# Batch 0 through the same half-size products as the other batches, its values in a tile of their own, and every step from one ordered list

## The chip, the cores and the metric

The kernel runs on one core of a Trainium2 chip, in one launch. The metric is the device time of that core in microseconds; the time before is the median of three runs. Profiles show one execution of the program, recorded by the hardware profiler. Engines: PE (TensorE matmuls; PEld its weight loads), DVE (VectorE), ACT (ScalarE), POOL (GpSimd, which also issues every load from device memory), SP (SyncE, which issues stores, copies inside SBUF and DMA transposes).

## The reference

A sparse attention over 4 batches, 8 heads, 768 tokens and 64 columns per head, then a feed-forward layer with a quick gelu (512 to 2048 to 512):

```python
k_sum = k.reshape(B, H, nb, block, D).max(axis=3)      # block 32: 24 blocks
v_sum = v.reshape(B, H, nb, block, D).mean(axis=3)
scores_l = scale * q @ k.T ; mask_l = abs(i - j) < 16
scores_s = scale * q @ k_sum.T + log(block)
a = softmax(concat([where(mask_l, scores_l, -1e9), scores_s]))
x = a @ concat([v, v_sum])                             # heads side by side: 3072 x 512
h = x @ w_in
out = (h * sigmoid(1.702 * h)) @ w_out
```

So each token attends to at most 31 neighbours and to 24 block summaries.

## The kernel before, in words

**Engines in order.** Every instruction goes through `_Ordered`, whose `call` (line 28) keeps it in program order on its engine. Nearly all rows of the profile therefore carry line 28, and groups are told apart by tile names. What stands first in the program stands first on its engine's queue.

**Layout.** A batch is 768 tokens in two halves of 384. Heads go in four pairs p. Keys of a pair lie turned in `kx` as 12 tiles of 128 columns: 64 own keys, 24 block maxima, 32 neighbours' keys, padding. Values lie in `vw` in the same 128 rows. `kx`, `qT` and `vw` exist twice, for even and odd batches. A pair's scores for one half are twelve matmuls into `ps_s` (a double PSUM bank), an exponential on ACT into `a_sb`, a mask product on DVE with `mk`; its values are twelve matmuls into `ps_av`, a reciprocal and a product on DVE into `x`; `x` is turned into `xT` by PE (`tx`, tile `ps_x`) or by a DMA transpose (`dx`).

**Values' rows.** The neighbours' rows of `vw` are copied from other rows of `vw` by SP (`halo_dmas`: four copies), the 24 block sums from `vs` by two more (`sum_dmas`). The sums come from matmuls with a selector `E` into `ps_vs` and five DVE instructions (`block_sums`).

**Feed-forward.** `ph` = 4 matmuls of 384 columns per 128 of the 2048 hidden units and half; ACT applies the gelu into `gT`. For batches 1 to 3 the second layer uses the Strassen-Winograd form: seven half-size products instead of eight, in `product`, eight matmuls of 256 columns each, for three row tiles t. Its left operands are `gT` and the sums `gs` (`g_sums`, four DVE instructions per column tile and batch), its right ones `w_out` and the differences `ws` (`w_sum`). Products gather in banks `poA`, `poB`, `poC`; copies `s` and results `osb` leave on DVE and ACT, and SP stores `osb`.

**Batch 0.** Half 0 starts from special tiles while loads are still coming: whole 128-key tiles for own keys (`s_own`), separate small matmuls for neighbours (`s_edges`) and blocks (`b_turn`). Then come its 16 hidden tiles (`ff_in`, first two by `ff_first`), and its second layer as plain full products (`ff_out`, tile `po`, 16 matmuls of 512 columns for each row tile). Half 1's scores and values stand between these (`beside0`), then half 1's hidden tiles with the turning of batch 1's keys and queries (`tk`, `tq`, tile `ps_t`), then its `ff_out` with batch 1's attention between. Its values are loaded straight into `vw[0]` by eight DMAs, the second half of q by eight more (`load_q1`).

**Loads.** POOL issues all loads in order; at most eight are under way, since each waits for the eighth before it. Batch 1's loads stand behind the masks and w_out, batch b+2's behind the first product of batch b's second layer or, for batch 2, behind batch 0's. Keys and queries of batches 2 and 3 are turned by DMA transposes on SP (`xk`, `xq`), after which DVE takes the block maxima (`rest_k`, tile `ks`) and fills the neighbours' and maxima's columns of `kx`.

**PSUM.** Eight banks: `pmm`, four single ones, and `psb`, two double ones, each pool handing out its buffers in turn. Ahead of them, for the start, three other pools of two.

**Order of the work around.** Batch b+1's attention stands between the products of batch b by hand-made tables, for example

```python
plan = {-1: ["s00", "s01"], 2: ["m00", "m01"], 3: ["s02", "s03"], 5: ["m02", "m03", "s10", "s11"],
        7: ["m10", "m11", "s12", "s13"], 9: ["m12", "m13"], 10: ["v00", "v01"], 11: ["d00"], ...}
```

where a number is a place among the products and s, m, v, d are scores, mask, values and the transpose of a half and a pair. The activation table is switched between the exponential and the gelu by `exp_soon` and `gelu_soon`.

## Time and profile before

| | |
|---|---|
| runs | 213.35, 217.09, 213.35 us; median 213.35 |
| the profiled execution | 215.52 us, of which the profile's span is 213.8 |
| granted TensorE clock | 1.0 throughout |
| matmuls | 2359, PE busy 203.4 us (95%) |
| DVE, ACT, POOL busy | 127.2, 122.6, 97.6 us |
| DMA | 27.74 MB in 99690 packets, 89280 of them under 512 B |
| activation table loads | 10, 1283 ns each |

A group's row gives the line, engine and operation, output and inputs, shapes and count; then the busy us, the mean ns of one, and the engine's idle time just before them with what ended it. Matmuls overlap, so a mean is longer than the distance between two. A timeline row gives start, length, engine and group. In the slices each digit is a fortieth of the span, 9 for 90% or more.

### The profile page before, as it was taken

Reading aid. Unit: us, or ns where it says so; the run is one execution under the profiler, and the core shown is the slowest. Engines: PE = TensorE matmul, PEld = TensorE weight load, DVE = VectorE, ACT = ScalarE, POOL = GpSimd, SP = SyncE. Lnnn points to the kernel's source line nnn. Section 1 sums busy time; section 2 is a strip of 40 time slices with the busy share of each in tenths; the row PEclk is TensorE's granted clock in tenths of the full one; section 3 lists DMA queues with packets and bytes.
Section 4 is the critical chain, followed back from the end, with each engine's and each line's share of the span. In section 5 each row is a group of like instructions: output and inputs, shape, how many; then the busy total and the mean of one; then the engine's idle time right before and its main releaser. Section 6 shows DMA issues by size and latency. Waiting matters only on the chain.

```text
span 213.8 us, 5822 instructions
## 1 busy us (share of the span) xinstructions
PE 203.4 (95%) x2359; PEld 138.1 (65%) x2359; DVE 127.2 (59%) x384; ACT 122.6 (57%) x233; POOL 97.6 (46%) x156
## 2 busy tenths in 40 slices
PE   7899997999999999999699999999999999999993
PEld 2657564556664566665578876666788866668882
DVE  4565783455974693299885735996667615444111
ACT  2374778157849726776664248768671467772220
POOL 7998897379899989179369300000000000000000
PEclk9999999999999999999999999999999999999999
DMA  5999999999999999999999997943023820000222
GB/s 62 157 157 200 199 207 174 186 151 217 145 78 160 180 156 134 150 183 138 152 160 206 164 254 138 182 71 79 0 101 88 161 98 3 0 0 0 101 98 100
DMA packets 99690, 27.74 MB, mean 130 GB/s; under 512 B 89280, under 2 KB 96720, under 8 KB 99664
## 3 DMA queue, kind: packets, MB, share of 16 engines
q0 software_dynamic: 74032, 13.64, 82.2%
q1 hardware_dynamic: 25632, 13.74, 31.2%
q8 instruction: 18, 0.29, 0.6%
q14 instruction: 8, 0.07, 0.1%
HBM read 27.26 MB, written 6.29 MB: 157 GB/s over the span
## 4 chain that ended last, share of the span: by engine, by line
PE 52%; DMA 17%; POOL 14%; DVE 10%; issue 3%; ACT 2%; POOLq 0%; DVEq 0%
PE ph L28 21%; PE poA L28 13%; PE poB L28 6%; DMA w_out_sb<-in_moe_w_out_dram 5%; POOL qb L28 5%; POOL vw L28 4%; DMA kx<-kb 4%; PE po L28 4%; DVE gs L28 4%; PE poC L28 4%; DMA w_in_sb<-in_moe_w_in_dram 3%; DMA qb<-in_q_dram 3%; PE ps_av L28 2%; POOL mk L28 2%; PE ps_s L28 2%
## 5 line engine op out<-in xcount | busy, mean ns | idle before, releaser
L28 PE MATMUL ph<-xT,w_in_sb 128*128 128x384 bf16 x512 | 86.4, 326 | 0.5 <-DVE xT L28 0.5
L28 ACT ACTIVATE gT<-ph 128x384 f16<-128x384 f32 x128 | 61.3, 491 | 25.9 <-PE ph L28 25.7
L28 PEld LDWEIGHTS <-w_in_sb 128*128 128x128 bf16 x512 | 49.3, 98 | 31.8 <-issue 0.6
L28 PEld LDWEIGHTS <-gT 128*128 128x128 f16 x312 | 29.2, 98 | 12.4 <-issue 0.7
L28 POOL DMA_DIRECT2D vw<-in_v_dram x44 | 31.5, 758 | 6.4 <-PE ps_s L28 1.7
L28 ACT ACTIVATE a_sb<-ps_s 128x768 bf16<-128x768 f32 x32 | 24.3, 806 | 15.1 <-PE ps_s L28 15.0
L28 PEld LDWEIGHTS <-gs 128*128 128x128 f16 x288 | 27.5, 98 | 4.6 <-issue 1.2
L28 DVE TENSOR_TENSOR gs<-gT 128x384 f16<-128x384 f16 x48 | 17.0, 354 | 22.0 <-ACT gT L28 21.9
L28 POOL DMA_DIRECT2D kb<-in_k_dram x28 | 22.9, 841 | 11.8 <-DMA kx<-kb 5.6
L28 POOL DMA_DIRECT2D qb<-in_q_dram x34 | 27.4, 839 | 1.6 <-DMA vw<-in_v_dram 1.1
L28 PE MATMUL po<-w_out_sb,gT 128*128 128x512 f16 x96 | 22.8, 380 | 0.0
L28 DVE TENSOR_TENSOR a_sb<-a_sb,mk 128x768 bf16<-128x768 bf16 x28 | 14.9, 555 | 7.9 <-ACT a_sb L28 7.1
L28 PE MATMUL poA<-ws,gs 128*128 128x256 f16 x144 | 18.7, 273 | 0.8 <-DVE s L28 0.8
L28 DVE TENSOR_TENSOR x<-ps_av,rc 128x384 bf16<-128x384 f32 x32 | 17.8, 558 | 1.1
L28 DVE TENSOR_REDUCE ks<-kx 128x24 bf16<-128x768 bf16 x12 | 11.4, 948 | 7.4 <-DMA kx<-kb 4.0
L28 ACT ACTIVATE s<-poA 128x256 f32<-128x256 f32 x14 | 5.4, 385 | 17.8 <-PE poA L28 17.4
L28 ACT ACT_TABLE_LOAD x10 | 12.8, 1283 | 1.0 <-PEq L1069 0.8
L28 DVE RECIPROCAL rc<-ps_av 128x6 f32<-128x6 f32 x32 | 6.0, 189 | 8.2 <-PE ps_av L28 7.9
L28 DVE TENSOR_TENSOR osb<-poC,s 128x256 f32<-128x256 f32 x9 | 3.8, 423 | 11.8 <-PE poC L28 10.0
L28 PE MATMUL poA<-ws,gT 128*128 128x256 f16 x72 | 9.3, 272 | 0.4 <-DVE osb L28 0.4
L28 PE MATMUL poA<-w_out_sb,gT 128*128 128x256 f16 x72 | 9.4, 273 | 0.0
L28 PE MATMUL poB<-ws,gs 128*128 128x256 f16 x72 | 9.4, 273 | 0.0
(88 smaller groups left out, 205.8 us busy)
## 6 DMA issues: line engine op xcount, KB each, us to landing
out_dram<-osb SPq DMA_DIRECT2D x23, 256.0 KB, 3.4
kb<-in_k_dram POOLq DMA_DIRECT2D x24, 96.0 KB, 6.2
qb<-in_q_dram POOLq DMA_DIRECT2D x24, 96.0 KB, 5.7
vw<-in_v_dram POOLq DMA_DIRECT2D x36, 64.0 KB, 5.2
w_out_sb<-in_moe_w_out_dram POOLq DMA_DIRECT2D x4, 512.0 KB, 10.7
w_in_sb<-in_moe_w_in_dram POOLq DMA_DIRECT2D x3, 512.0 KB, 10.3
vw<-vs SPq DMA_DIRECT2D x6, 198.0 KB, 4.7
kb<-in_k_dram POOLq DMA_DIRECT2D x4, 192.0 KB, 5.3
```

What stands on the lines that cost most here:

```text
L28: r = f(*a, **kw)
```

## The change

1. **Batch 0's second layer** uses `product` like the others: both halves' hidden tiles first, then 21 half-size products. `g_sums` takes one or two column tiles at a time.
2. **Batch 0's values** are loaded by four DMAs into a tile `v0n`; DVE copies the rows that half 1 needs into `vw[0]` (`own0`). The late half of q is loaded as the early one is, three tokens to a row, by two DMAs, and turned by the same helper. Half 1's keys are laid out by instructions over all four pairs at once, some on POOL (`late_own`, `late_halos`, `late_rows`). The scores' mask is put into PSUM ahead of the scores (`s_mask`).
3. **PSUM** is six pools of one buffer, four single banks (0 to 3) and two double ones (4, 5), and every step names its bank; 40, 41, 50, 51 are halves of the double ones.
4. **Every step** stands in the string `ORDER`: a step's name, its numbers, its engine (d, a, g) or bank. The tables, the loops and `beside` go. Loads, copies, exponentials and sums are steps of their own; some copies out of PSUM move between DVE and ACT. The exp and gelu switches for batch 0 become one each.

```diff
-    pidle = first.enter_context(tc.tile_pool(name="pidle", bufs=2, space=bass.MemoryType.PSUM))
...
+    psum = [ctx.enter_context(tc.tile_pool(name=f"ps{i}", bufs=1, space=bass.MemoryType.PSUM)) for i in range(6)]
-    def load_q1(h):
...
-        pool.dma_start(out=qb2["late"][:, h // 2, :, h % 2],
-                       in_=q[0, h, HALF:S].rearrange("(a p) d -> p a d", p=128))
+    def load_q0(half, g):
...
+        pool.dma_start(out=qb2[half][:, 4 * g:4 * g + 4].rearrange("p h r d -> p h (r d)"),
+                       in_=q[0, 4 * g:4 * g + 4, half * HALF:half * HALF + HALF]
+                       .rearrange("h (p r) d -> p h (r d)", r=JH))
+    def load_v0(p):
+        pool.dma_start(out=v0n[:, 2 * p:2 * p + 2, :, 0:D].rearrange("p h j d -> p (h j) d"),
+                       in_=v[0, 2 * p:2 * p + 2].rearrange("h (j p) d -> p (h j) d", p=128))
+    def own0(e):
+        r = slice(64 * e, 64 * e + 64)
+        dve.tensor_copy(out=five(0)[r, JH - e:NJ, e, :, 0:D],
+                        in_=v0n[r, :, JH - e:NJ, 0:D].rearrange("p h j d -> p j h d"))
+    def late_own(e, eng):
+        flat = kxs[0].rearrange("p i t c -> p (i t c)")
+        kf = kn.rearrange("p i s -> p (i s)")
+        eng.tensor_copy(out=at(flat, 256 * JH + 192 * e, [[NQ * 128, NP], [256, JH], [1, 64]]),
+                        in_=at(kf, HALF + 64 * e, [[S, NP], [128, JH], [1, 64]]))
-    def ff_out(u, ms, part):
...
-            pe.matmul(out=po, lhsT=gT[u % 2][:, nt, ms * 128:(ms + 1) * 128],
-                      rhs=w_out_sb[:, nt, :], start=(nt == 0), stop=(nt == NT - 1))
```

Parts of the order around batch 0's half 1 (Q and Qc q turn and copy, s and e scores and exponential, f hidden tile, G the switch to gelu, g gelu, vo and vr own rows and sums, ha and sd SP's copies, m mask, v and n values, t and c turn of x), the middle of batch 0's products with batch 1's sums and the release of batch 2's loads (gate, lk, lv, lq), and the first steps of batch 1's hidden tiles with the transposes (xk, xq), key maxima (xm) and key copies (kh, kr):

```
f.0.0.k01.2 f.0.1.k01.3 Q.1.1.0 Qc.1.2.a Qc.1.3.d mf s.0.1.1.42 e.1.1 f.0.0.k23 s.0.1.2.52 e.1.2 f.0.2.k0123.1
f.0.1.k23 s.0.1.3.42 e.1.3 f.0.3.k0123.0 ... f.0.7.k0123.41 G g.0.0 g.0.1 g.0.6 g.0.7 vo.0 vo.1 vr ha.0.0.3
g.0.2 g.0.3 sd.0.0.3 g.0.4 ha.0.3.3 sd.0.1.3 m.1.0 ha.0.1.3 ha.0.2.3 ow.1 ck.1 ... f.0.8.k0123.2 m.1.1 m.1.2 m.1.3
g.0.8 f.0.9.k0123.3 g.0.9 f.0.10.k0123.1 g.0.10 v.0.1.0.40 v.0.1.1.41 n.1.0 n.1.1 f.0.11.k0123.0 g.0.11 v.0.1.2.50
...
p.1.5.1 x.1.5.a ha.1.0.0 ha.1.2.0 ha.1.3.0 vm.1.42 vb sd.1.0.0 sd.1.1.0 gate lk.2.0 lk.2.1 lv.2.2.0 lv.2.2.1 lv.2.3.0
lk.2.3 lv.2.5.0 lv.2.5.1 lk.2.2 lk.2.4 lk.2.5 ha.1.1.0 lk.2.7 lv.2.0.1 lv.2.0.0 lk.2.6 ...
g.0.9 xk.0.0.0 xk.0.0.1 xk.0.1.0 xk.0.1.1 xq.0.0 xq.0.1 f.1.0.k0123.2 g.1.0 ... gs.0.2.3 xm.0.0 kh.0.0.d kr.0.0.d ...
```

## The prediction

> **What bounds the kernel now.** I read the page's busy shares and slices first, then the costliest groups, then PE's timeline by stage, then the waits.

> ```profile
> PE 203.4 (95%) x2359; PEld 138.1 (65%) x2359; DVE 127.2 (59%) x384; ACT 122.6 (57%) x233; POOL 97.6 (46%) x156
> ...
> PE   7899997999999999999699999999999999999993
> ...
> PEclk9999999999999999999999999999999999999999
> DMA  5999999999999999999999997943023820000222
> ```

> TensorE is the bound: 203.4 of 213.8 us, always at the full granted clock. The DMA engines are full until 128 us. They do not stop PE, but a transfer issued in that time lands late.

> ```profile
> L28 PE MATMUL ph<-xT,w_in_sb 128*128 128x384 bf16 x512 | 86.4, 326 | 0.5 <-DVE xT L28 0.5
> ...
> L28 PE MATMUL po<-w_out_sb,gT 128*128 128x512 f16 x96 | 22.8, 380 | 0.0
> ...
> L28 PE MATMUL poA<-w_out_sb,gT 128*128 128x256 f16 x72 | 9.4, 273 | 0.0
> ...
> vw<-vs SPq DMA_DIRECT2D x2, 99.0 KB, 5.3
> ...
> vw<-vw SPq DMA_DIRECT2D x3, 49.5 KB, 5.7
> ```

> Matmuls overlap, so their mean ns is a latency. The cadence comes from the timeline's starts: 48 ph in 7.96 us are 0.163 each; 16 po in 3.63 are 0.217; eight poA start 0.873 after the eight before them, 0.109 each. The last two lines are copies inside SBUF for batch 0's second half, issued on SP; they land 5.3 and 5.7 us after issue.

> ```profile
> 21.79 0.87 PE L28 MATMUL ph<-xT,w_in_sb 128*128 128x384 bf16 x4
> ...
> 36.00 3.63 PE L28 MATMUL po<-w_out_sb,gT 128*128 128x512 f16 x16
> 39.56 0.57 PE L28 MATMUL ps_av<-vw,a_sb 128*64 128x65 bf16 x24
> ...
> 46.86 0.50 PE L28 MATMUL ps_x<-wide,x 128*128 128x128 bf16 x6
> ...
> 81.16 7.15 PE L28 MATMUL ph<-xT,w_in_sb 128*128 128x384 bf16 x43
> ...
> 105.61 1.03 PE L28 MATMUL poA<-ws,gs 128*128 128x256 f16 x8 [0.77 <-DVE s L28]
> ```

> Input products of half 0 start at 21.8. Half 1's values (ps_av) at 39.6 need the copies above, and 16 po hide their flight. At 47.2 half 1 is turned, with 40 of half 0's 48 po done. Batch 1's input products start at 79.5, its products at 102.9.

> ```profile
> DVE ks L28 <- DMA kx<-kb: 4.0, 1, 4.0
> ...
> PE ps_s L28 <- DVE vs L28: 0.9, 1, 0.9
> ...
> PE poA L28 <- DVE s L28: 0.8, 1, 0.8
> ...
> PE ps_vs L28 <- DMA vw<-in_v_dram: 0.5, 1, 0.5
> ```

> VectorE waits 4.0 us for the key transposes of batch 2, runs 14 us without a gap (91.0 to 105.1), and PE waits 0.9 and 0.8 at the end of that. These are most of PE's named waits after the start.

> **The change, part by part.** The sum is made against the profiled span of 213.8 us. That execution took 215.5; the runs shown have a median of 213.35, so differences are carried over to that median.

> *Products of batch 0.* 96 matmuls of 512 columns (96 x 0.217 = 20.8 us) become 7 x 8 x 3 = 168 of 256 (168 x 0.109 = 18.3): **-2.5**. VectorE gets batch 0's sums gs: six in pairs of 768 columns (the mask product of that size takes 0.555) and two single ones, 12 x 0.555 + 8 x 0.354 = 9.5 us, beside the 8 ws sums of 0.68 (5.5 us). They lie in half 1's input products, 16 x 0.65 + 3 x 0.33 = 11.4 us, with 2.1 us of product and turn cover (p.1.1, p.0.1, tk.3). 15.0 us of VectorE against 13.5 of cover: it overruns some 1.5, but product 5 needs only the first of the last sums. I take 0.3 on the path, bounds 0 and 1.5. Without the cover all 9.5 would be on it.

> *The start, to the point where batch 0's half 1 is turned.* The first DMAs keep their order, so the first half ends as before: last norm at 22.0 to 22.8 us. POOL now does kx copies (768 elements: from the 0.43 of its 288-element copy I take 0.9; in all 2.8 us) ahead of the third w_in load. They wait for the last turned keys (13.5) and maxima (17.8), not for the end, and end near 19; mask building follows and ends near 28 (its 27.3 before). So the first half-1 scores are not held, and input products start at 23.5 instead of 21.8, for a q turn, three x turns and a score group now stand ahead. Then to the end of the 11th input tile: 11 x 0.65 + q turn 0.46 + 3 score groups at 0.23 and 0.1 of entry each + 0.7 where the second q turn waits for the x copies behind an exponential = 9.3, that is 32.8. Here half 1's values want their rows. VectorE writes own rows and sums only after the last q copy (25.9): 0.68 + 0.9 + 4 x 0.24, done at 28.4. Behind that SP issues five more copies at 0.6 to 0.8 each (last one near 31.2), landing 5.2 to 5.8 later among the w_out loads: **36.8**. PE stands 4 us; its own queue, all the other input tiles, is behind it, and so are the two values' norms on VectorE and everything later. Then four value groups (1.1), five input tiles (3.25), two turns (0.66): 41.8. Before, 47.2 less the 40 po (8.7) is 38.5. So **+3.3**, bounds -0.7 (no wait) and +4.5 (w_in's third chunk 1 us late too).

> [...]

> *From there to batch 1's input products.* Work in both: 16 input tiles, 8 turns of k and q, sums, 8 score and 8 value groups, 3 x turns. Before, the extra over those sums is 79.5 - 47.2 - 30.4 = 1.9 (the 0.5 for the v load among it). After: 8 entries of 0.1, the 0.3 above, and 0.7 where values of batch 1 stand 6.3 us behind the sums whose copies need 1.5 on VectorE and 4.7 to land: 1.8. **-0.1**, bounds -1.9 and +2. The half-q loads in longer runs (2048 fewer packets) and four v loads instead of eight shorten the DMA queue; PE waited 0.5 and 1.1 on it, counted above, bounds 0 and -1.6.

> *Batch 1's products.* Before, 24.8 us for 18.3 + 1.85 + 1.8 of work. The first key transposes again stand behind a store, and batch 2's loads start at 66 (64.5 before), the keys now mixed with v loads (15th instead of 8th issue). They land near 91 as before. VectorE's 14 us shrink by 1.0, for its gs come in pairs, and copies out of PSUM move to ACT: **-0.9**, bounds 0 and -1.85 (both waits gone).

> *Batches 2 and 3.* The 0.2 waits for osb go with these moves: **-0.3**, bounds 0 and -1. PSUM: six pools with the same four single and two double banks, so no more buffering than before; the two table loads saved (10 to 8, 1.28 each) are on ACT, 57% busy: 0 on the path; without that cover 2.6. The tail is unchanged.

> Sum: -2.5 + 3.3 - 0.1 - 0.9 - 0.3 = **-0.5**, a span of 213.3 and a median of **212.9**.

> **The rivals.**

> *The rows for half 1 are there in time* (faster). If the SBUF copies land in 2.8 us, as batch 1's larger ones did by the DMA issues from 60 to 68 us, 2.9 of the 4 us go; if the q turn's wait, which holds up VectorE's rows, is missing, another 0.7; with the waits of batch 1 gone too (0.9) the time is 208.4. For it: a short first DMA queue. Against: all six copies of this very stage took over 5 us.

> *Batch 2's keys become the bound* (slower). Place: the four key transposes in batch 1's input products. VectorE needs 9.5 us after the last pair (two maxima with copies 3.0, sums gs 4.0, block sums 1.5, a first share of the last sums 1.0), and PE wants product 5 near 103.2. So it decides when the last pair lands after 93.7, and each us beyond is a us of PE, once in batch 1 and again in batch 2, whose loads are mixed in the same way. Loads drain 1.7 us later and the transposes are served with them; the last pair can be issued when the 15th load has landed (66.2 + 15 x 0.79 + 5.5 = 83.5), 2.5 apart by the longest issue, and lands 8.8 later by the slowest of them, near 94.8, and with the 1.7 near 96.5: 2.8 us twice, 218.5. For it: VectorE's 4.0 us wait above. Against: before, transposes issued from 80.6 to 86.0 overlapped.

> *The half-size products give nothing* (no change). If VectorE's sums for batch 0 cost the full 1.5 overrun and ACT's copies lag, the 2.5 are given back: 214 to 215. For it: 15.0 against 13.5. Against: PE's needs come in steps.

> **How the numbers follow.** My forecast has 0.38, the faster rival 0.31, the slower one 0.19, the third 0.12. A measurement of this kernel tells about 2% from no change, 4.3 us: under 209.1 is faster, over 217.6 slower. The forecast and the third case are within: 0.50. The faster rival gives 0.31, the slower 0.19. The forecast's own range, by the start's and the middle's bounds halved, is 210 to 216. To leave out no more than 2 in 10 the range must reach into both others: 206.5 (208.4 less the middle's lower bound, 1.9) to 218.0.

> **What would show it.** 168 more matmuls of 256 columns and no po row; PE idle of some 4 us ahead of the first ps_av with 64-column tiles, named after a DMA vw, near 33 us; input products from 23.5; half 1 turned near 42; batch 1's input products near 80, its products at 102 to 103. No such idle would prove the start wrong; a "DVE ks <- DMA kx" wait over 5 us, with PE waiting on gs, would prove the slower rival.

## The result, and the profile after

The changed kernel takes 221.41 us (median of 6 runs, 219.72 to 223.96) against 214.66 for the kernel before beside it (6 runs, 213.35 to 217.99): a ratio of 1.029, 95% interval 1.024 to 1.034. It is slower; 212.9 was forecast, and 221.4 lies above the range given. Ratios, here and below, leave out executions more than 1.5% above the fastest of their kernel; medians do not. The profiled execution took 222.04 us, its span is 220.1.

First the page of the changed kernel: busy time by engine, PE's busy tenths and PE's granted clock in 40 slices of 5.5 us, and the DMA share.

```profile
PE 203.4 (92%) x2416; PEld 145.7 (66%) x2416; DVE 135.3 (61%) x364; ACT 119.2 (54%) x233; POOL 93.6 (43%) x150
...
PE   7778893999999499999999998999999999999994
...
PEclk9999997699999959999999999999999999999999
DMA  6999999999907999999999999994011840000222
```

PE is as long busy as before although batch 0's products are 2.5 us less work, and there are two dents in its row (the 3, and the 4 in the middle), each with a dent of the clock in the same slice or the next. Before, the clock had none. The waits of PE name what makes the dents in its own row (us in total, times, longest):

```profile
PE ps_av L28 <- DMA vw<-vw: 7.7, 2, 4.0
```

PE's timeline (start, us, operation, tiles, count, idle time before it and what ended it) shows both places:

```profile
27.23 5.58 PE L28 MATMUL ph<-xT,w_in_sb 128*128 128x384 bf16 x32
36.78 0.96 PE L28 MATMUL ps_av<-vw,a_sb 128*64 128x65 bf16 x24 [3.97 <-DMA vw<-vw]
37.67 1.46 PE L28 MATMUL ph<-xT,w_in_sb 128*128 128x384 bf16 x4
...
73.57 0.22 PE L28 MATMUL ps_av<-vw,a_sb 128*64 128x65 bf16 x1
77.48 0.84 PE L28 MATMUL ps_av<-vw,a_sb 128*64 128x65 bf16 x23 [3.69 <-DMA vw<-vw]
78.25 1.89 PE L28 MATMUL poB<-ws,gs 128*128 128x256 f16 x8
...
88.46 1.46 PE L28 MATMUL ph<-xT,w_in_sb 128*128 128x384 bf16 x8
```

The first wait is the forecast one: half 1's values of batch 0, 3.97 us, ended at 36.78. The second stands at batch 1's first values, 3.69 us; before, PE reached these without a wait, at 71.42. Behind each, work runs at half speed: four `ph` in 1.40 us up to the next group (0.65 before), eight `poB` in 1.82 (0.87 before). Batch 1's input products start at 88.46, where 80.1 was forecast and 79.53 was the time before.

The granted clock in windows of 0.5 us (window, its length, busy us of PE, PEld, DVE, ACT, POOL, then PEclk, DMA share, GB/s):

```profile
35.50:36.00 0.50, 0.00 (x0) 0.00 (x0) 0.00 (x0) 0.00 (x0) 0.00 (x0) 0.63 1.22 236
36.00:36.50 0.50, 0.00 (x0) 0.00 (x0) 0.00 (x0) 0.00 (x0) 0.00 (x0) 0.50 1.23 205
...
42.00:42.50 0.50, 0.50 (x4) 0.25 (x3) 0.00 (x0) 0.00 (x0) 0.44 (x2) 0.54 2.41 153
...
76.50:77.00 0.50, 0.00 (x0) 0.00 (x0) 0.00 (x0) 0.00 (x0) 0.00 (x0) 0.59 1.31 279
...
83.00:83.50 0.50, 0.50 (x6) 0.44 (x5) 0.07 (x1) 0.23 (x1) 0.50 (x2) 0.58 2.04 129
```

The windows between these show 0.50, those outside 1.00. So a mean of 0.63 over 0.5 us is read as 0.13 us at 1.0 and the rest at 0.5: the clock falls at 35.63. Read alike, it is back at 42.46, falls at 76.59 and is back at 83.42. Each time it is low for 6.83 us, of which PE works 5.68 and 5.94: half of that, 2.8 and 3.0 us, is lost. So the waits cost 7.7 us and the low clock, called half clock below, 5.8.

What makes the second wait is on SP's queue:

```profile
65.54 0.88 SPq L28 DMA_DIRECT2D out_dram<-osb  x2
66.61 2.71 SPq L28 DMA_DIRECT2D vw<-vw  x3
69.43 1.27 SPq L28 DMA_DIRECT2D vw<-vs  x2
70.74 0.94 SPq L28 DMA_DIRECT2D vw<-vw  x1
```

The halo copies of batch 1 stand behind two stores that can only go at 65.5, when batch 0's first sums have left PSUM; the last halo stands behind the block sums' copies too and lands near 77.4. PE wants the rows at 73.8. Before, these copies stood ahead of the stores, and the values (first line) came 5 us behind the last one's issue:

```profile
71.42 0.57 PE L28 MATMUL ps_av<-vw,a_sb 128*64 128x65 bf16 x24
...
61.83 2.68 SPq L28 DMA_DIRECT2D vw<-vw  x4
64.61 1.56 SPq L28 DMA_DIRECT2D vw<-vs  x2
```

### The profile page after: what moved, and what is told of

Its sections match the earlier page's. It is cut to its first block, busy times and chain, and to the rows that moved or that the text cites. A ratio compares the mean times of both kernels' runs of the same rounds, so it can differ in the third digit from the quotient of the medians.

```text
span 220.1 us, 5893 instructions
## 1 busy us (share of the span) xinstructions
PE 203.4 (92%) x2416; PEld 145.7 (66%) x2416; DVE 135.3 (61%) x364; ACT 119.2 (54%) x233; POOL 93.6 (43%) x150
## 3 DMA queue, kind: packets, MB, share of 16 engines
q0 software_dynamic: 71824, 13.64, 77.9%
## 4 chain that ended last, share of the span: by engine, by line
PE 74%; DMA 13%; POOL 6%; DVE 3%; SPq 2%; issue 1%; ACT 0%; POOLq 0%; DVEq 0%
PE ph L28 36%; PE poA L28 17%; PE poB L28 9%; DMA vw<-vw 5%; DMA w_in_sb<-in_moe_w_in_dram 5%; PE poC L28 4%; PE ps_av L28 3%; DMA out_dram<-osb 3%; PE ps_s L28 2%; POOL v0n L28 2%; SPq L28 2%; POOL qb L28 1%; POOL kb L28 1%; PE ps_t L28 1%; PE ps_x L28 1%; DVE vs L28 1%
## 5 line engine op out<-in xcount | busy, mean ns | idle before, releaser
L28 PE MATMUL ph<-xT,w_in_sb 128*128 128x384 bf16 x512 | 88.0, 331 | 0.0
L28 ACT ACTIVATE gT<-ph 128x384 f16<-128x384 f32 x128 | 58.9, 494 | 33.6 <-PE ph L28 33.2
L28 PEld LDWEIGHTS <-w_in_sb 128*128 128x128 bf16 x512 | 49.6, 99 | 32.6 <-issue 1.6
L28 PEld LDWEIGHTS <-gs 128*128 128x128 f16 x384 | 37.0, 100 | 5.2
L28 DVE TENSOR_TENSOR gs<-gT 128x768 f16<-128x768 f16 (+1 forms) x40 | 18.5, 474 | 22.3 <-ACT gT L28 22.0
L28 POOL DMA_DIRECT2D kb<-in_k_dram x28 | 23.4, 841 | 18.4 <-DMA kx<-kb 9.9
L28 PEld LDWEIGHTS <-gT 128*128 128x128 f16 x288 | 27.6, 98 | 4.4 <-issue 0.8
L28 ACT ACTIVATE a_sb<-ps_s 128x768 bf16<-128x768 f32 x32 | 24.5, 808 | 5.5 <-PE ps_s L28 5.4
L28 POOL DMA_DIRECT2D vw<-in_v_dram x36 | 25.2, 759 | 2.2 <-DMA w_out_sb<-in_moe_w_out_dram 1.6
L28 PE MATMUL poA<-ws,gs 128*128 128x256 f16 x192 | 25.8, 279 | 0.0
L28 POOL DMA_DIRECT2D qb<-in_q_dram x28 | 23.2, 865 | 2.0 <-DMA vw<-in_v_dram 2.0
L28 ACT ACTIVATE s<-poA 128x256 f32<-128x256 f32 x18 | 6.9, 385 | 22.5 <-PE poA L28 20.1
L28 DVE TENSOR_TENSOR x<-ps_av,rc 128x384 bf16<-128x384 f32 x32 | 17.8, 558 | 1.1
L28 DVE TENSOR_TENSOR a_sb<-a_sb,mk 128x768 bf16<-128x768 bf16 x28 | 14.6, 553 | 3.7 <-ACT a_sb L28 3.6
L28 PE MATMUL ps_av<-vw,a_sb 128*64 128x65 bf16 x336 | 8.5, 210 | 7.7 <-DMA vw<-vw 7.7
L28 PEld LDWEIGHTS <-a_sb 128*64 128x64 bf16 (+1 forms) x360 | 8.3, 122 | 10.5 <-issue 9.4
L28 DVE RECIPROCAL rc<-ps_av 128x6 f32<-128x6 f32 x32 | 6.1, 189 | 14.3 <-PE ps_av L28 14.1
L28 PE MATMUL poB<-ws,gs 128*128 128x256 f16 x96 | 13.3, 285 | 0.0
L28 PE MATMUL poA<-ws,gT 128*128 128x256 f16 x96 | 12.4, 273 | 0.6 <-DVE osb L28 0.6
L28 POOL COPY kx<-kx 128x80 bf16<-128x80 bf16 (+1 forms) x12 | 3.5, 336 | 21.4 <-DMA kx<-kb 17.4
L28 PE MATMUL poC<-w_out_sb,gT 128*128 128x256 f16 x96 | 12.6, 274 | 0.0
L28 PE MATMUL poB<-w_out_sb,gs 128*128 128x256 f16 x96 | 12.5, 273 | 0.0
(95 smaller groups left out, 215.8 us busy)
```

The source lines that it names most:

```text
L28: r = f(*a, **kw)
```

## The experiments

All are copies of the changed kernel with words of the list moved, unless said otherwise. The ratio is that to the kernel before, with its 95% interval. T, T2, R1 and R2 are the theories that an expectation names. What is read from a profile is read from one execution.

### The waits, each and both, and the waits filled

**e1, batch 1's rows earlier.**

```diff
 e.0.1 p.0.3
+ha.1.0.0 ha.1.2.0 ha.1.3.0 ha.1.1.0 vm.1.42 vb sd.1.0.0 sd.1.1.0
 x.1.1.a ... o.0.0.0.0.2 ... o.0.0.1.0.2 ... x.1.5.a
-ha.1.0.0 ha.1.2.0 ha.1.3.0 vm.1.42 vb sd.1.0.0 sd.1.1.0
 gate ... lk.2.5
-ha.1.1.0
```

> Only the second wait is taken away: batch 1's block sums and its six in-SBUF row copies are issued ahead of batch 0's first stores (sums on TensorE one score group earlier). Theory T (the changed kernel loses its time in two TensorE waits for row copies, 4.0 and 3.7 us, and in the half clock of about 6 us that follows each, 2.6 us each): the idle of 3.7 us ahead of batch 1's values shrinks below 1 us, the granted clock there stays at 1.0, and the time is 6.3 us less than the changed kernel's, near 215. Rival R1 (the half clock has nothing to do with standing still): only 3.7 us go, near 217.7, and the half clock still shows near 77 us. Rival R2 (the time is lost in the half-size products and the single list, and the waits only move): within 2 us of the changed kernel.

Measured 219.87 us, ratio 1.020 (1.012 to 1.027). The second wait is gone, but the sums now stand ahead of other work on DVE, and PE waits 0.64 us for `vs` and 1.79 for `osb` a little earlier, with half clock from 68.25 to 71.67. The first wait is as it was (3.95 us). The test moved too much; m1 below moves less.

**e2, batch 0's rows earlier.** The memsets `ow.0 cv.0 cvs` go into DVE's time between 8.1 and 11.3 us, and:

```diff
 xc.0.a ... Q.1.0.42
+vo.0 ha.0.0.3 ha.0.1.3
 Qc.1.0.a Qc.1.1.d
+vo.1 ha.0.2.3 ha.0.3.3 vr sd.0.0.3 sd.0.1.3
 ... g.0.7
-vo.0 vo.1 vr ha.0.0.3
 g.0.2 g.0.3
-sd.0.0.3
 g.0.4
-ha.0.3.3 sd.0.1.3
 m.1.0
-ha.0.1.3 ha.0.2.3
```

> Only the first wait is taken away: VectorE clears batch 0's value tile in an idle gap before 13 us, and writes own rows and sums right after the first half's last norm, 3.4 us earlier, so that the six row copies are issued from 23.4 to 27.5 us instead of 26.8 to 31.9. Theory T: the copies land near 32.5 to 33, the idle of 4.0 us at 32.8 us is below 1 us, no half clock after it, and the time is 5.5 to 6.6 us less, near 215 to 216. R1: 3 to 4 us less, and a half clock still shows near 36 to 42 us. R2: within 2 us of the changed kernel.

Measured 215.83 us, ratio 1.002 (0.998 to 1.005). The first wait and its half clock are gone, and 5.6 us with them: most of what the change had lost. The second wait is now in two parts, on PE's timeline:

```profile
69.71 0.19 PE L28 MATMUL ps_av<-vw,a_sb 128*64 128x65 bf16 x1 [1.89 <-DMA vw<-vs]
71.39 0.84 PE L28 MATMUL ps_av<-vw,a_sb 128*64 128x65 bf16 x23 [1.49 <-DMA vw<-vw]
```

One matmul between them did not help: read from windows as above, the clock falls at 70.76 and is back at 77.59.

**e3, both edits together.**

> Both edits together. T: both idles and both stretches of half clock are gone, 12 to 13 us less than the changed kernel, near 208.5 to 209.5, and faster than the kernel before by 2 to 3%. R1: 7 us less, near 214, with half clock left. R2: 217 or more; and if batch 2's keys take over as the bound once the rest is earlier, 211 to 213 with a wait of VectorE for kx over 4 us.

Measured 216.87 us, ratio 1.011 (1.006 to 1.015): no better than e2, and 8 us above what T gave. No wait for row copies is left; others came, on PE's timeline:

```profile
58.74 0.25 PE L28 MATMUL ps_vs<-vw,E 64*32 64x128 bf16 x7 [0.46 <-DMA vw<-in_v_dram]
59.43 0.30 PE L28 MATMUL ps_vs<-vw,E 64*32 64x128 bf16 x16 [0.44 <-DMA vw<-in_v_dram]
...
61.38 0.78 PE L28 MATMUL ps_s<-qT,kx 64*128 64x64 bf16 x24 [0.66 <-DVE vs L28]
63.70 1.87 PE L28 MATMUL poB<-ws,gs 128*128 128x256 f16 x8 [1.54 <-DVE osb L28]
```

The sums now wait for batch 1's v loads, which land near 59.4, and DVE stands behind the sums. The clock falls at 61.47, after no single wait of more than 0.7 us.

**e4, the waits filled.** Seventeen matmuls of 512 columns on `w_in_sb` into a free bank ahead of `v.0.1.0.40`, fifteen ahead of `v.1.0.0.50`.

> The waits stay, but TensorE does not stand still in them: 17 products of 512 columns on data at hand (3.7 us, their results are used by nothing) ahead of batch 0's second-half values, 15 (3.3 us) ahead of batch 1's values. The row copies land when they did. T: granted clock 1.0 throughout, so 2.6 us less after each wait, 5 us in all, near 216, though not a word of the order is moved. R1: the clock still falls, time unchanged within 1 us, near 221. R2: no less, rather more than the changed kernel.

Measured 218.89 us, ratio 1.014 (1.006 to 1.022). PE's timeline at both places:

```profile
34.84 3.83 PE L28 MATMUL ps_h<-w_in_sb 128*128 128x512 bf16 x17 [0.34 <-ACT gT L28]
38.59 0.57 PE L28 MATMUL ps_av<-vw,a_sb 128*64 128x65 bf16 x24
...
72.70 3.40 PE L28 MATMUL ps_h<-w_in_sb 128*128 128x512 bf16 x15
76.03 0.57 PE L28 MATMUL ps_av<-vw,a_sb 128*64 128x65 bf16 x24
```

### Where the rest of the gain goes

**e5, all rows early, sums in place.** Batch 0's rows as in e2, and:

```diff
 x.0.3.a
+ha.1.0.0 ha.1.2.0
 o.0.0.0.0.2
+ha.1.3.0 ha.1.1.0
 x.0.4.a
-o.0.0.1.0.2
 ... x.1.5.a
-ha.1.0.0 ha.1.2.0 ha.1.3.0
 vm.1.42 vb sd.1.0.0 sd.1.1.0
+o.0.0.1.0.2
 gate ... lk.2.5
-ha.1.1.0
```

> From the kernel with batch 0's rows early (215.8 us, where TensorE still stands 1.9 and 1.5 us ahead of batch 1's values and 6.8 us of half clock follow): the four halo copies of batch 1 go ahead on SyncE's queue, two before and two after batch 0's first store, the sums stay where TensorE and VectorE make them. Theory T: the last copy is now one of the sums', issued near 64 us and landing near 69.5 to 70, where TensorE wants it at 67.8: a wait of 1.5 to 2 us is left. [...] R2 (nothing to be had from the rows): 215.8.

Measured 214.49 us, ratio 0.999 (0.995 to 1.003): level with the kernel before, and 0.5 above the 214 expected for a clock that falls at this wait too. Its profiled execution kept the clock at 1.0 over one wait, now for the sums, and took 213.72, where 211 to 212 were expected for a clock that holds:

```profile
70.04 0.56 PE L28 MATMUL ps_av<-vw,a_sb 128*64 128x65 bf16 x23 [2.62 <-DMA vw<-vs]
```

Four others had a mean clock of 0.992 and took 0.5 to 0.9 us more than it. The clock is not all: one at 0.999 took 215.51.

**e6, batch 1's first values two products later.** `p.2.5.1 x.2.5.a p.2.6 x.2.6.a` go ahead of `v.1.0.0.50`; turning and copying follow.

> The same, and batch 1's first values two products of batch 0 (1.75 us) later in TensorE's order, the transposes and their copies with them. T: no wait over 0.7 us from 25 us on, granted clock 1.0, and both the 3.4 us of waits and the 3.1 us of half clock of the kernel with batch 0's rows early are gone: 209 to 210.5, 2% or more under the kernel before. If batch 2's keys or sums take over as the bound now that all comes 6 us earlier, 211 to 212.5, with waits named after gs or vs near 100 us. R2: 215 or more.

Measured 217.07 us, ratio 1.009 (1.004 to 1.014), a clear miss. The wait is still 1.55 us, batch 1's input products start at 78.35 (e5: 78.38), and a new wait comes in batch 2, for a DMA transpose that lands late:

```profile
129.08 0.50 PE L28 MATMUL ph<-xT,w_in_sb 128*128 128x384 bf16 x2 [1.29 <-DMA xT<-x]
```

**e7, e6 with full products for batch 0.** All `gs` of batch 0 go; each `p` of batch 0 becomes 4 or 8 matmuls of 512 columns into `po`, and ACT copies `po` to `osb`.

> The same again, but batch 0's second layer as 96 full products of 512 columns instead of 168 half-size ones, copied out by ScalarE, and without VectorE's sums gs for batch 0 (8 ws sums stay). The computed output is the same. T: the half-size products are worth what the count of columns says, so this is 2.2 to 2.5 us slower than the kernel with values later, near 212. R2 (half-size products give nothing, since VectorE's 9.5 us of sums cost what TensorE gains): no difference, or faster.

Measured 217.29 us, ratio 1.011 (1.001 to 1.021): 0.2 above e6, not 2.2 to 2.5. Batch 1's input products start at 78.43 (e6: 78.35). PE has 2.5 us more to do there and waits 1.9 us less. Beside rows that come when they come, the half-size products buy waiting.

**m2, the changed kernel with full products for batch 0**, nothing else changed (as in e7).

> The changed kernel with the half-size products of batch 0 alone taken back: 96 full products of 512 columns, copied out by ScalarE, without VectorE's sums gs for batch 0 (the 8 ws sums stay); rows, queues and waits as in the changed kernel. TensorE reaches batch 1's values 1.8 us later (75.5 us), the block sums stand 0.9 us later. If the gain of the half-size products goes into the wait for the rows: the second wait falls by 0.9 us to 2.8, and batch 1's input products come 1 to 1.6 us later than the changed kernel's 88.5, not 2.5 later: 221 to 223. If they are worth their count: wait unchanged at 3.7 and 224.

Measured 219.81 us, ratio 1.023 (1.016 to 1.030): not slower than the changed kernel. The second wait:

```profile
75.92 0.54 PE L28 MATMUL ps_av<-vw,a_sb 128*64 128x65 bf16 x23 [1.09 <-DMA vw<-vw]
```

It is 2.6 us shorter: PE comes 1.0 later, and the last copy lands 1.6 earlier. That copy was issued at 70.9, in the changed kernel at 70.7, and took 4.9 us to land instead of 6.6; no run shows whether the products have a part in that. Behind it the clock stays at 1.0, and behind the first wait it is low from 37.47 to 40.88 only, which costs 1.7 us instead of 5.8 for both. So it is 61.4 us from the first to batch 1's input products, against 65.4: 2.5 more of work, 2.7 less waiting, 4.1 less lost to the clock. Why the clock was low for 3.41 us here and for 6.83 behind the changed kernel's first wait, no run shows; the other two cancel, with the help of that quicker copy. The cleaner pair is e6 and e7.

**m1, the halos alone on SP's queue.** The moves of e5 without those of e2; the second store goes behind the sums' copies.

> The changed kernel with one edit on SyncE's queue alone: batch 1's four halo copies go ahead, two before and two after batch 0's first store; its sums, its values and all of batch 0's rows stay. In the changed kernel the last halo copy stands behind two stores, three halos and both sums' copies, is issued at 70.7 us and lands at 77.4. Theory T: the sums' copies (70.7 us at the latest) are now last and land near 76.2, so the second wait falls from 3.7 to 2 to 2.7 us and the first (4.0 us, with its half clock) stays; the half clock behind the second comes in some runs only, as in the kernel with all rows early: 217.5 to 220. If the place of the halos on the queue is not what sets the second wait: 3.5 us of wait and 221.

Measured 221.51 us, ratio 1.027 (1.019 to 1.035). The wait is of the size T gave:

```profile
76.80 0.57 PE L28 MATMUL ps_av<-vw,a_sb 128*64 128x65 bf16 x23 [2.09 <-DMA vw<-vs]
```

So the place of the halos on SP's queue set 1.6 us of the second wait, and the sums' copies the rest. The median did not fall, and is what was expected if the halos' place did not matter. The profiled execution took 225.4 and is read for this stage only: batch 1's input products come 60.0 us after the first ones instead of 65.4, most of it by less half clock (3.4 us of it behind the first wait, none behind the second), and batch 2 gives the gain back in this execution, with 1.81 and 0.75 us of wait for `xT`. Where the others lost it was not seen.

**e9, e5 with nine products of 512 columns in the wait.**

> From the kernel with all rows early and the sums where they were (214.5 us; its profiled run at clock 1.0 stands 2.6 us ahead of batch 1's values): nine products of 512 columns on data at hand (2.0 us, results used by nothing) fill that wait, nothing else is changed. Its runs so far took 213.1 to 213.7 at a mean granted clock of 1.0, 214.2 to 214.6 at 0.992 and 215.4 to 216.9 at 0.984. [...]

If TensorE's idle time in that wait is what brings the clock down, nearly all runs were expected at 0.998 or above, with a median of 213.2 to 213.8 us; if it falls for another reason, the same spread of clocks and 214.5.

Measured 214.98 us, ratio 1.001 (0.996 to 1.006). The clock did what the first of these says: ten of its twelve executions had 0.997 or above, in e5 three of ten. The time did not: the profiled execution, at clock 1.0, waits 1.45 us for `vs` and 0.7 each for `gs` and `s` from 102 us on.

**e10, batch 1's q in two loads with long runs**, sums and rows half a product group earlier than in e5.

```diff
-lk.1.6 lq.1.0 lq.1.1 lk.1.7 lq.1.2 ... lq.1.7
+lk.1.6 lk.1.7 L4.0 L4.1
+pool.dma_start(out=qb2[g] (p h (r d)), in_=q[1, 4g:4g+4].rearrange("h (p r) d -> p h (r d)", r=NJ))
```

> Is the wait of 2.6 us that is left set by batch 1's loads, so that TensorE's gain from the half-size products can't come out? Batch 1's q is loaded by 2 DMAs of four heads in runs of six rows (1024 packets) instead of 8 DMAs in single rows (6144 packets), and put back in order by the copies out of PSUM; its block sums and rows are issued half a product group earlier, as that now finds its values landed. GpSimd issues 6 loads of 0.82 us less ahead of the values, so these land near 54.5 to 55 instead of 59.4, the rows near 66 to 67, where TensorE wants them at 67.4. If the loads set it (T): no wait over 0.7 us ahead of batch 1's values, batch 1's input products from 75.5 to 76 instead of 78.4, its products from 98 instead of 100.7; behind that batch 2's loads, which start 2 to 2.5 us earlier, take over as the bound: 211.5 to 212.8, 1% under the kernel before. If not (the rows' own 5.5 us of landing or the sums set it): a wait of 1.5 us or more stays, and 213.5 to 214.5.

Measured 218.25 us, ratio 1.014 (1.005 to 1.024). The wait ahead of batch 1's values is gone, as T said; batch 1's input products come 54.5 us after the first ones, in e5 55.3. But batch 2's loads started later (65.5 instead of 62.9): the gate ahead of them stands on POOL behind a key copy that waits for block maxima, and DVE now makes these behind the sums. The profiled execution took 220.7, 2.5 above the median, so its later stages are not read; where the 218.25 come from is not shown.

**l1, l2, l3: lighter loads** of q and k for batches 2 and 3, in e5, in the kernel before and in the changed kernel:

```diff
-pool.dma_start(out=t2[g][:, i, :, hh], in_=x[b, h].rearrange("(a p) d -> p a d", p=128))
+pool.dma_start(out=t2[g] (flat)[:, o:o + NJ * D], in_=x[b, h].rearrange("(p r) d -> p (r d)", r=NJ))
```

> The kernel with all rows early (214.5 us, no better than the kernel before although its first two waits are eased), but batches 2 and 3 load q and k in runs of six rows without putting them back in order: the same bytes from memory in a sixth of the packets. Left out is the order of the rows of q and k in batches 2 and 3, so those batches compute attention over permuted rows; every instruction of the engines stays. Theory T2 (with the first waits eased, the loads of batches 2 and 3 set the pace from batch 1's input products on, which is where the rest of the expected gain went): the waits for vs, gs and s near 102 to 106 us and for xT near 126 us go, 2 to 3.5 us less, 211 to 212.5. If TensorE's own work sets the pace there: 214 to 215.

> The kernel before with the same lighter loads for batches 2 and 3 (again their rows of q and k stay permuted). T2: the waits of 0.9 us for vs and 0.8 us for s near 103 to 106 us go and what collides with the loads, 1.5 to 2.5 us less, 212 to 213, so that the half-size products, early rows and list are worth 0.5 to 1.5 us more than nothing once loads don't bind. If the loads bind neither: no change, 214.5.

> The changed kernel with the same lighter loads. T: it lies behind its loads by the 13 us of row waits and half clock, which come before batch 2's loads are wanted, so it gains least of the three, at most 1.5 us: 219.5 to 221. If loads are its cause instead: 216 or less.

Measured 213.65 (ratio 0.994, 0.990 to 0.999), 214.89 (0.999, 0.995 to 1.003) and 220.15 us (1.026, 1.018 to 1.034). The medians gave less than T2 asked, except in l3. The stage that the loads were to bind did as T2 said: from batch 1's input products to PE's end l1 takes 127.65 us (e5: 130.2), l2 128.8 (before: 130.6) and l3 the same as l1, 127.65 (changed kernel: 128.4). In l1 and l2 the front gave it back: l1's profiled execution waits 2.0 and 1.3 us for the rows, with half clock (mean clock 0.990), and l2's comes to batch 1's input products 1.3 us later than the kernel before.

PE's milestones in the profiled executions, in us:

| kernel | first input products | batch 1's input products | from there to PE's end | mean clock |
|---|---|---|---|---|
| before | 21.8 | 79.5 | 130.6 | 1.000 |
| changed | 23.1 | 88.5 | 128.4 | 0.969 |
| e2 | 23.7 | 82.5 | 128.0 | 0.984 |
| e5 | 23.1 | 78.4 | 130.2 | 1.000 |
| e6 | 23.0 | 78.4 | 132.1 | 0.999 |
| e7 | 23.1 | 78.4 | 133.6 | 0.992 |
| l1, light loads | 23.5 | 80.9 | 127.7 | 0.990 |
| l2, before, light loads | 21.1 | 80.8 | 128.8 | 0.998 |
| l3, changed, light loads | 23.0 | 87.5 | 127.7 | 0.969 |

With the loads as they are, kernels that come to batch 1's input products at 78.4 to 79.5 take 130.2 to 133.6 us from there, those that come at 82.5 and 88.5 take 128.0 to 128.4; the order is not strict, for e3 comes at 81.6 and takes 129.9, e4 at 84.4 and takes 130.0. No kernel here that computes the whole beats the kernel before by what can be told: e5 and e9 are level with it, and l1 computes something else in batches 2 and 3.

## Why the prediction was wrong, point by point

- **Start: place and size of the first wait right, its price not.** Input products started at 23.1 (23.5 forecast), PE stood 3.97 us (4) until 36.78 (36.8), and SP's copies for batch 0 took 5.4 to 5.7 us to land (medians of the page). Half 1 was turned at 44.41 instead of 41.8. The 2.6 between are the half clock (2.8 lost), for which the sum had no term. e4 shows it: the wait filled, and this stage 2.5 us shorter.
- **The middle: the step that failed.** Its term "0.7 where values of batch 1 stand 6.3 us behind the sums" measured 3.69. It followed the sums' copies and left out the halo copies, which stand behind two stores and, the last of them, behind the sums on the same queue. m1 and e5 show the order's share, 1.6 us, and that the sums' copies alone leave 2.1 to 2.6. So their path was too short as well: the forecast had 1.5 on VectorE and 4.7 to land, 6.2 against a distance of 6.3, from which the 0.7 does not follow; in m1 it is 9.3 us from the sums to the values (67.49 to 76.80), 2.2 of them on VectorE and 6.5 for the later copy to land. Before, the values stood 10.0 us behind the sums, in the changed kernel 7.0. With 3.0 of half clock behind the wait, this stage took 44.1 us instead of the forecast 38.3, and both terms, 3.0 + 3.0, are the difference within 0.2.
- **Together** these are 8.8 us (2.8 + 3.0 + 3.0), and 8.4 with the start 0.4 earlier than forecast: batch 1's input products come at 88.46 against 80.1. They are more than the whole error in the profiled span, 6.8 (220.1 against 213.3), for the rest of the sum was pessimistic: batch 1's input products and products took 45.1 us against 46.7 before, -1.6 (forecast -0.9), batches 2 and 3 -0.6 (forecast -0.3). In the median the error is 8.5, mostly since the forecast set out from a median of 213.35 in three runs of the kernel before, which has 214.66 in six.
- **The products of batch 0, -2.5: right as work, wrong as time.** 168 matmuls at 0.109 us are there, but e7, and m2 with the help of a quicker copy, show that taking them back costs nothing that can be told: PE comes sooner to rows that land no sooner. The third rival had this outcome, by VectorE's overrun; that was not the mechanism, for in the changed kernel PE nowhere waits for `gs`.
- **The faster rival** supposed half 1's rows in time. In e2 and e5 they are, with 215.83 and 214.49, not 208.4: batch 1's rows still come late there. Its v loads land near 59.4 (e3's lines), sums and copies bring the rows to 70, and behind that the loads of batches 2 and 3 take a share (l1 and l2, 1.8 to 2.6 us of that stage).
- **The slower rival**, batch 2's keys, had the right sign for another reason: in the changed kernel PE waits at most 0.6 us anywhere behind 84 us, and VectorE's longest wait for a key transpose is 2.8 us, not over 5. Waits for what DVE makes for batch 2, 0.6 to 1.5 us each, show in the kernel before and where the front is faster (e4, e9).
- **The range:** 210 to 216 was to come from halved bounds, but only the lower ones are halved; with the upper ones halved too (1.2 and 2.1) it ends at 214.5. The time lies beyond either, by what the sum left out.
- **What was not weighed** is the low clock behind a wait. In the changed kernel it stood at 0.50 for 6.83 us from 35.63 and again from 76.59, and 2.8 and 3.0 us were lost; in m2, at a first wait of 3.86 us, it was low for 3.41 (37.47 to 40.88), and 1.7 were lost.

Open is what brings the clock down, for the idle time alone does not decide it. In e3 it fell at 61.47, with waits of 0.46, 0.44 and 0.66 us ahead of it and 1.56 us of idling in all from 58.06 on. In m1 it stayed at 1.0 over a wait of 2.09 us, in e5's profiled execution over one of 2.62.

## What to carry to other kernels

A forecast wait of TensorE is priced with its length and with what half clock may follow: here 1.7 to 3 us behind each wait of 3.1 us or more (changed kernel, e1, m1, m2, l3), none behind single waits of 2.1 and 2.6 (m1, e5), but 1.6 to 3.1 us behind some short waits close together (e1, e2, e3, l1). On a hand-ordered queue, list every entry ahead of the last transfer that a stage needs, stores that wait for results above all, before sizing the wait. Fewer TensorE cycles ahead of data that arrive at a fixed time were no gain here (0.2 us between e6 and e7): look for what sets that time first.

## What the runs showed of the hardware that was not expected

- Where the clock fell, it was low for 3.4 us (e1, 37.53 to 40.95 and 68.25 to 71.67; m2) or 6.8 us (changed kernel; e2, 70.76 to 77.59; e3, 61.47 to 68.30), and the length of the wait does not tell which: 3.4 us behind waits of 3.95 (e1) and 3.86 (m2), 6.8 behind waits of 3.97 and 3.69 (changed kernel). In e2 PE worked from 71.39 on, and the clock stayed low for another 6.2 us.
- Executions of one program differ in the clock: e5 took 213.1 and 213.7 us at a mean clock of 1.0, 214.2 to 214.6 at 0.992 and 215.4 to 216.9 at 0.983 to 0.984, but also 215.5 at 0.999.
- Runs of six rows in place of one made little difference to the time in l3: the software queue had 71824 packets in the changed kernel, which took 77.9% of the span, and has 51344 in l3 as an estimate from the edit (32 loads of 128 runs in place of 768 rows). The medians, 221.41 and 220.15 us, differ by less than their runs do.
